# A shorter conv for one more block, with its weights loaded sooner, its softmax pieces and bands moved, and a warm-up in short matmuls

## Chip, cores, metric

One core of one Trainium2 chip. The metric is the device time of one execution in microseconds (us). All runs compared here are in the fast state. Times are medians; ratios are computed as the mean time of one kernel's fast runs over that of the other's of the same rounds, so they are not quite the ratios of the medians that are quoted.

## The reference, cut to what matters

A dynamic convolution (softmax weights over 7 taps, per token and head) feeds a feed-forward layer with a squared ReLU:

```python
w = softmax(weight_gen, axis=-1)                 # [8, 4096, 8 heads, 7 taps]
x_unf = x_pad[:, idx].reshape(B, S, K, H, 24)    # the last 7 tokens, 24 channels a head
x = einsum('bshk,bskhg->bshg', w, x_unf)         # -> 32768 tokens x 192
h = np.maximum(x @ w_in, 0.0)                    # 192 -> 2048
out = (h * h) @ w_out                            # 2048 -> 192
```

## The kernel before

Tokens go in blocks (the first two of 512, then of 1024); blocks count from 0, and the eighth is block 7. Names used below: a *unit* is 128 of the 2048 hidden channels for the block's 1024 tokens (`h`, six matmuls; relu on ScalarE; square `g` on VectorE for two units together). A *half sum* is 32 matmuls of the second layer into two PSUM banks `o0` and `o1`; after every second one ScalarE copies `o0` to SBUF and VectorE adds `o1` (`o_sb`). The *conv* of the next block multiplies x by *bands* (`bd`), which VectorE makes from the softmax weights (`wr`). A *piece* of softmax is a sum, a reciprocal and four or eight multiplications on VectorE, behind an exp on ScalarE. The kernel fixes by hand the order in which each engine gets its work, and this text holds that order:

```python
steady        = "MuMuuu" * 3 + "MuuuMCu"          # u unit, M half sum, C conv of the next block
steady_spread = "MuMuuu" * 2 + "MuCMuuu" + "MuMuuu"
...
TIMES = {                                          # softmax pieces: (block, before which unit)
    ...
    (1, 2): ((4, 2), (5, 1), (5, 15)),
    (2, 0): ((6, 1), (6, 15), (7, 0)),
    ...
}
...
us = {4: (7, 9), 6: (7, 9)}.get(j, (5, 9) if small else (1, 5))   # bands: before which units
if j + 1 >= FIRST_SPREAD:                          # FIRST_SPREAD = 8
    us = (1, 5)
```

The conv has two forms. A head has 24 channels and this kernel uses the array in groups of 32 columns, so in the long form a group straddles two heads and is written twice: 120 matmuls a block. In the short ("spread") form each head has a group of its own, and the 8 spare rows hold parts of the last two heads, filled in by DMA afterwards: 80 matmuls, but w_in must lie in a permuted order (`w_p`, loaded and then copied crosswise), and the conv must come early enough for the fill of y. Before, blocks 8 and later use it.

```python
copy(out=y[:, k0 : k0 + 2], in_=yp)                # ScalarE for one pair of slots, VectorE for the other
for p0 in range(0, P, 32):                         # four fill DMAs a block
    ...
    nc.sync.dma_start(out=y[p0 + G : p0 + 32, 0:NK], in_=y[r0 : r0 + G, NK])
```

The warm-up keeps TensorE busy until the first softmax weights are there:

```python
def spin(n):
    for i in range(n):
        nc.tensor.matmul(out=wp, lhsT=warm[:, 0:P], rhs=warm, start=True, stop=True)   # 512 columns
...
spin(21)
```

The softmax here doesn't subtract the row's maximum and nothing guards it: scores larger than these inputs give would overflow.

Of the kernel before, what the change touches and what calls it, by code (L numbers as in the profile page):

```python
# [9 lines left out]
def kernel(  # L10
# [26 lines left out]
    nc = tc.nc  # L37
# [3 lines left out]
    B, S, D = x.shape  # L41
    H, KK = weight_gen.shape[2], weight_gen.shape[3]
# [1 line left out]
    Dm = moe_w_out.shape[1]  # L44
    HK = H * KK
    G = D // H
    SPREAD = H - 2
    FIRST_SPREAD = 8
    HP = H // 2

    P = 128
    TB = 512
# [10 lines left out]
    RT = 64  # L63
    NK = D // RT
# [37 lines left out]
    PARTS = {0: (8, 8, 8, 8), 1: (8, 8, 16), 2: (16, 16)}  # L102
    v_big = const.tile([P, R + 2 * HALO, HP, SL, 2], f16, name="v_big")
    v_first = [
# [38 lines left out]
    def load_w_spread():  # L143

        def rows(head, k=None):
            a = moe_w_in[G * head : G * (head + 1)]
            return a if k is None else a.rearrange("(r k) c -> k r c", k=NK)[k]

        for e in (0, 1):
            for k in range(NK):  # L150
                for a, n, src in (
                    (0, G, rows(2 * k + e)), (G, RT // 2 - G, rows(SPREAD + e, k))
                ):
                    if k < 2:
                        p0 = RT * k + 32 * e + a
                        nc.gpsimd.dma_start(
                            out=w_p[p0 : p0 + n, :, 0, 0:NQ],
                            in_=src.rearrange("r (q c) -> r q c", q=WQ),
                        )
                    else:  # L160
                        for half in (0, 1):
                            p0 = RT * half + 32 * e + a
                            nc.gpsimd.dma_start(
                                out=w_p[p0 : p0 + n, :, 0, NQ:],
                                in_=src.rearrange("r (q h c) -> h r q c", q=WQ, h=2)[half],
                            )
# [124 lines left out]
    def rows(ap2d, t0, width):  # L291

        return bass.AP(
            tensor=ap2d.tensor, offset=ap2d.offset + t0 * width,
            ap=[[width, P], [STEP * width, NT], [1, width]],
        )
# [175 lines left out]
    def st_conv_spread(j):  # L472

        s0, n = BLOCKS[j]
        y = p_y.tile([P, NK + 1, TB], f16, name="y")
        y_t[j] = y
        for ks in ((NK, NK - 1), (0, 1)):
            yp = ps_h.tile([P, 2, TB], f32, name="yp", tag="h")
            k0 = min(ks)
            for k in ks:  # L480
                for i in range(NT):
                    a, b = bounds[i], bounds[i + 1]
                    for half in (0, 1):
                        s = s0 + half
                        hi = a + (STEP if tile_start(s, i) == starts[i] else b - a)
                        bd = bd_t[s][:, H * a : H * hi].rearrange(
                            "p (g c e) -> p g e c", g=HP, e=2
                        )
                        for e in (0, 1):
                            head = 2 * k + e  # L490
                            p0 = RT * half + 32 * e
                            c0 = min(G * head, D - 32)
                            nc.tensor.matmul(  # L493
                                out=yp[p0 : p0 + 32, k - k0, a:b],
                                lhsT=x_t[s][:, i, c0 : c0 + 32],
                                rhs=bd[:, head // 2, e, 0 : b - a],
                                start=True,
                                stop=True,
                                skip_group_check=True,
                                tile_position=(0, p0),  # L500
                            )
            copy = nc.vector.tensor_copy if k0 == 0 else nc.scalar.copy
            copy(out=y[:, k0 : k0 + 2], in_=yp)  # L503
        for p0 in range(0, P, 32):
            head = SPREAD + p0 // 32 % 2
            r0 = p0 + G * head - min(G * head, D - 32)
            nc.sync.dma_start(out=y[p0 + G : p0 + 32, 0:NK], in_=y[r0 : r0 + G, NK])

    def st_conv(j):

        if j >= FIRST_SPREAD:
            return st_conv_spread(j)
# [49 lines left out]
    def st_unit(j, u):  # L562

        w = w_p if j >= FIRST_SPREAD else w_i
        h = ps_h.tile([P, 2, TB], f32, name="h", tag="h")
# [91 lines left out]
    with nc.allow_low_precision("fp16 matmul pipeline"), tc.manual_schedule():  # L657
# [18 lines left out]
        warm = const.tile([P, TB], f16, name="warm")  # L676
# [3 lines left out]
        for v in v_first:  # L680
            nc.vector.memset(v, 0.0)

        wp = ps_o.tile([P, TB], f32, name="wp", tag="o0")

        def spin(n):
            for i in range(n):
                nc.tensor.matmul(out=wp, lhsT=warm[:, 0:P], rhs=warm, start=True, stop=True)

        s0, s1, s2 = parts[:3]
        spin(21)  # L690
        row_select()
        band_mask()
        s0.load(nc.sync)
# [35 lines left out]
        for q in range(4):  # L729
# [10 lines left out]
        plans = {  # L740
            0: "u P B1 u u u E1 C S1 u u M u u",
            1: "L3 u u B2 M E2 B3 u M E2 u u S2 S2 u M u C u M",
            2: "L4 u u u E3 M u u u M B4 u u u u M B5 S3 u u u u M u C E3 u",
            3: "L5 L6 u u u M S3 u u u M u M E4 u u B6 u M u M B7 u u u E4 M u M C S4 u",
        }


# [3 lines left out]
        def at(j, u, kind, *args):  # L751
# [5 lines left out]
        TIMES = {  # L757
            (1, 0): ((3, 15), (4, 0)),
            (1, 1): ((4, 15), (5, 0)),
            (1, 2): ((4, 2), (5, 1), (5, 15)),  # L760
            (2, 0): ((6, 1), (6, 15), (7, 0)),
            (2, 1): ((7, 9), (8, 9)),
            (3, 0): ((9, 9), (10, 0), (10, 9), (11, 9)),
# [2 lines left out]
        def exp_time(j, u):  # L766

            if u == 0:
                return j - 1, 12
            return j, {1: 0, 2: 1, 7: 3, 8: 4, 9: 4, 13: 12, 15: 8}[u]  # L770

        for n, s in enumerate(parts):
            k = n - min(m for m, p in enumerate(parts) if p.b == s.b)
# [4 lines left out]
        for n, s in enumerate(parts[4:], 4):  # L778
            b, f = s.b, s.fb
            k = n - min(m for m, p in enumerate(parts) if p.b == b)  # L780
# [8 lines left out]
        for j in range(len(plans), NBLK - 1):  # L789
            a = BLOCKS[j + 1][0]  # L790
            small = [p for p in parts if p.fb <= j + 1][-1].r == FIRST
            us = {4: (7, 9), 6: (7, 9)}.get(j, (5, 9) if small else (1, 5))
            if j + 1 >= FIRST_SPREAD:
                us = (1, 5)
            for n, u in enumerate(us):
                at(j, u, "B", a + n)
        for j in range(len(plans), NBLK):
            plan, u = [], 0
            for step in steady_spread if j + 1 >= FIRST_SPREAD else steady:
                if step == "u":  # L800
# [18 lines left out]
        def soft(s):  # L819
            lo, hi = next(s.softs)  # L820
            s.total(lo, hi)
            s.recip(lo, hi)
            s.scale(lo, hi, nc.vector)
            if hi < s.rh:
                return
            if s.r == FIRST:
                move_rows(s)
                after = parts[parts.index(s) + 1]
                if after.b == s.b and after.r > FIRST:
                    s.store(nc.sync)  # L830
            else:
                s.store(nc.sync)
                stored.add(s)
                for w in [w for w in waiting if w[0] is s]:
                    waiting.remove(w)
                    load_rows(w[1])
# [21 lines left out]
        for j in range(NBLK):  # L858
            if j + 2 < NBLK:
                load_rows(j + 2)  # L860
            if j == 1:
                for q in range(WQ):
                    cross_w_in(q)
            u = 0
            for step in plans[j].split():
                kind, n = step[0], int(step[1:] or 0)
                if kind == "u":
                    st_unit(j, u)
                    u += 1
                elif kind == "M":  # L870
                    next(mm2)
                elif kind == "C" and j + 1 < NBLK:
                    st_conv(j + 1)
                    if j == 0:
                        x_load(3)
                    elif j + 2 < NBLK:
                        for k in range(BLOCKS[j + 2][0], sum(BLOCKS[j + 2])):
                            x_load(k)
                    if j == 5:
                        load_w_spread()  # L880
                    elif j == 6:
                        cross_w_spread()
                elif kind == "E":
                    parts[n].exp(*next(parts[n].exps))
                elif kind == "S":
                    soft(parts[n])
                elif kind == "B":
                    st_bands(n)
                elif kind == "P":
                    select_rows(1, s0, ROW_ORDER[4:], (o1,))  # L890
                    copy_rows(1, ROW_ORDER[4:])
                elif kind == "L":
                    parts[n].load(nc.sync)


        j = NBLK - 1
# [44 lines left out]
```

## Time and profile before

| | before |
|---|---|
| time, median of 3 runs | 731.79 us (731.56 to 731.87) |
| span of the profiled run | 730.0 us |
| TensorE / VectorE / ScalarE busy | 99% / 86% / 84% |
| conv of block 7, start to next start | 1.53 us (120 matmuls); of block 8: 1.07 us (80) |
| a later block | 22.1 us |

Busy time says only that TensorE is the bound. What a change is worth is read from the order of time: where TensorE stands, and how long before that moment the engine that must release it had finished. The lines are in the prediction.

### The profile page before, as it was taken

The page shows a single profiled execution, that of the slowest core. Times are in us where ns is not written, and L with a number is a line of the kernel's source. Part 1 is how long each engine was busy: PE and PEld are TensorE (multiplying, and loading weights), DVE is VectorE, ACT ScalarE, POOL GpSimd, SP SyncE. Part 2 cuts the span into 40 slices and gives each one's busy share as a digit, 9 for nine tenths or more (in the row PEclk, how much of TensorE's full clock was granted, in tenths as well). Part 3 has the DMA queues.
Part 4 walks back from the last instruction along what each step waited for, and adds up shares of the span by engine and source line. Part 5 has one row for each costly group of instructions (what it writes and reads, how often), then busy time and mean ns, then how long its engine had stood idle before and what let it go on. Part 6 is the DMA issues. An engine that isn't in the chain of part 4 may idle for free.

```text
span 730.0 us, 30988 instructions
## 1 busy us (share of the span) xinstructions
PE 724.1 (99%) x14053; PEld 528.0 (72%) x14053; DVE 626.8 (86%) x836; ACT 612.2 (84%) x733; POOL 99.8 (14%) x145
## 2 busy tenths in 40 slices
PE   8999999999999999999999999999999999999998
PEld 4657788777777777777777777777777777777777
DVE  7998998998898988888988888988889988778753
ACT  5999888888888888888888888888888888888883
POOL 8131223321001100011001010010000110001000
PEclk9999999999999999999999999999999999999999
DMA  9555455685345452455432554343544325444012
GB/s 202 118 105 115 82 96 105 132 149 129 86 66 138 90 92 59 82 117 124 76 64 61 136 104 88 56 77 116 107 84 86 57 52 119 66 87 78 30 45 68
DMA packets 125984, 68.30 MB, mean 94 GB/s; under 512 B 85321, under 2 KB 122140, under 8 KB 125340
## 3 DMA queue, kind: packets, MB, share of 16 engines
q0 software_dynamic: 46192, 19.43, 22.9%
q1 hardware_dynamic: 79516, 46.79, 22.4%
q8 instruction: 110, 1.80, 1.1%
q14 instruction: 22, 0.18, 0.1%
q10 hardware_dynamic: 144, 0.10, 0.0%
HBM read 50.18 MB, written 28.70 MB: 108 GB/s over the span
## 4 chain that ended last, share of the span: by engine, by line
PE 98%; ACT 1%; DVE 0%; DMA 0%; issue 0%
PE o L621 47%; PE h L572 44%; PE yp L493 4%; PE h L557 2%; PE yp L527 1%; DMA wg<-in_weight_gen_dram 0%; PE yp L455 0%; ACT y L538 0%; DVE v_first L260 0%; PE pr L372 0%; ACT t L586 0%; DVE ssum L245 0%; ACT ex L238 0%; DVE rcp L252 0%; ACT wr L381 0%
## 5 line engine op out<-in xcount | busy, mean ns | idle before, releaser
L586 ACT ACTIVATE t<-h 128x1024 f16<-128x1024 f32 x512 | 496.4, 1026 | 60.3 <-PE h L572 58.8
L621 PEld LDWEIGHTS <-g 64*128 64x128 f16 (+1 forms) x8032 | 344.3, 94 | 55.0 <-issue 2.2
L621 PE MATMUL o<-w_o,g 64*128 64x192 f16 (+1 forms) x8032 | 380.1, 243 | 0.1
L590 DVE TENSOR_TENSOR g<-t 128x2048 f16<-128x2048 f16 (+1 forms) x287 | 307.4, 1105 | 30.1 <-ACT t L586 29.9
L572 PE MATMUL h<-y,w_p 64*128 64x512 f16 x2400 | 291.7, 376 | 0.0
L572 PEld LDWEIGHTS <-w_p 64*128 64x128 f16 x2400 | 113.9, 94 | 94.7
L395 DVE TENSOR_TENSOR bd<-wr,mask 128x4160 f16<-128x4160 f16 (+4 forms) x90 | 149.6, 1686 | 1.3 <-ACT wr L381 0.7
L637 DVE TENSOR_TENSOR o_sb<-o,o_sb 128x384 f32<-128x384 f32 x123 | 68.4, 556 | 61.1 <-ACT o_sb L635 60.1
L321 POOL DMA_DIRECT2D xt<-in_x_dram x63 | 52.6, 839 | 415.3 <-PE yp L493 362.5
L635 ACT COPY o_sb<-o 128x384 f32<-128x384 f32 x129 | 61.6, 477 | 45.9 <-PE o L621 45.1
L572 PE MATMUL h<-y,w_i 64*128 64x512 f16 x576 | 70.6, 376 | 0.3 <-ACT t L586 0.3
L572 PEld LDWEIGHTS <-w_i 64*128 64x128 f16 x576 | 30.3, 94 | 22.2 <-issue 1.6
L493 PEld LDWEIGHTS <-xt 128*32 128x32 f16 x2000 | 24.6, 95 | 10.6 <-issue 10.6
L260 DVE TENSOR_TENSOR v_big<-ex,rcp 128x112 f16<-128x112 f32 (+5 forms) x180 | 29.9, 237 | 1.7 <-DMA vd<-v_big 0.7
L503 DVE CAST y<-yp 128x1024 f16<-128x1024 f32 x25 | 30.4, 1218 | 0.0
L493 PE MATMUL yp<-bd,xt 128*32 128x104 f16 (+1 forms) x2000 | 28.4, 210 | 0.0
L238 ACT ACTIVATE ex<-wg 128x560 f32<-128x560 f32 (+4 forms) x38 | 25.9, 682 | 1.9 <-DMA wg<-in_weight_gen_dram 1.9
L245 DVE TENSOR_REDUCE ssum<-ex 128x80 f32<-128x560 f32 (+4 forms) x38 | 25.3, 666 | 1.3 <-ACT ex L238 1.3
L503 ACT CAST y<-yp 128x1024 f16<-128x1024 f32 x25 | 25.2, 1007 | 0.0
L252 DVE RECIPROCAL rcp<-ssum 128x80 f32<-128x80 f32 (+4 forms) x38 | 22.8, 600 | 1.3
L311 POOL DMA_DIRECT2D xt<-in_x_dram x7 | 3.9, 554 | 120.9 <-PE yp L493 109.4
L355 POOL DMA_DIRECT2D wr<-v_first x24 | 12.9, 560 | 25.1 <-DVE v_first L260 13.6
(41 smaller groups left out, 115.1 us busy)
## 6 DMA issues: line engine op xcount, KB each, us to landing
out_dram<-o_sb SPq DMA_DIRECT2D x63, 384.0 KB
xt<-in_x_dram POOLq DMA_DIRECT2D x42, 240.0 KB, 4.7
wg<-in_weight_gen_dram SPq DMA_DIRECT2D x4, 1064.0 KB
xt<-in_x_dram POOLq DMA_DIRECT2D x21, 192.0 KB, 5.2
wr<-vd SPq DMA_DIRECT2D x38, 80.0 KB
vd<-v_big SPq DMA_DIRECT2D x5, 512.0 KB
y<-y SPq DMA_DIRECT2D x100, 24.0 KB
wg<-in_weight_gen_dram SPq DMA_DIRECT2D x3, 616.0 KB
```

The costliest lines, as they stand in the source:

```text
L238: nc.scalar.activation(out=self.ex[:, lo:hi].rearrange("p r g k e -> p (r g) k e"), in_=self.wg[:, lo:hi].rearrange("p r (g e) k -> p (r g ...
L260: eng.tensor_tensor(out=bass.AP(tensor=v.tensor, offset=v.offset + lo * H * SL + lo % SL * 2 + g * SL * 2, ap=[list(v.ap[0]), [H * SL + 2, ...
L321: eng.dma_start(out=dst[:, first:last], in_=ap)
L395: nc.vector.tensor_tensor(out=bd_t[j][:, H * lo : H * (lo + len(tiles) * n)].rearrange("p (g m c) -> p g m c", g=shape[1], c=2 * SL), in0= ...
L493: nc.tensor.matmul(out=yp[p0 : p0 + 32, k - k0, a:b], lhsT=x_t[s][:, i, c0 : c0 + 32], rhs=bd[:, head // 2, e, 0 : b - a], start=True, sto ...
L503: copy(out=y[:, k0 : k0 + 2], in_=yp)
L572: nc.tensor.matmul(out=h[:, half], lhsT=w_in_chunk(w, u, slot, half), rhs=y_t[j][r0 : r0 + RT, k], start=(slot == 0), stop=(slot == NK - 1 ...
L586: nc.scalar.activation(out=t1[:, e], in_=h, func=ActF.Relu)
L590: nc.vector.tensor_tensor(out=g[:, a : e + 1], in0=t1[:, a : e + 1], in1=t1[:, a : e + 1], op=AluOp.mult)
L621: nc.tensor.matmul(out=oo[:, cc * Dm : (cc + 1) * Dm], lhsT=g[r0 : r0 + n, cc * P : (cc + 1) * P], rhs=w_o[r0 : r0 + n, fc, :], start=(fc ...
L635: nc.scalar.copy(out=o_sb, in_=o[0][:, c])
L637: nc.vector.tensor_tensor(out=o_sb, in0=o[1][:, c], in1=o_sb, op=AluOp.add)
```

## The change

Intent: take the short conv for block 7 too (40 matmuls fewer). That needs `w_p` a block sooner, the conv of block 7 after unit 8 of block 6 and therefore its bands at units 4 and 6, and for these the third softmax piece of part (1,2) at unit 11 of block 5 so that its rows are stored in time. Besides: an exp of the fourth part moves from before the last unit of block 2 to behind the second unit of block 3 (three units later; the recorded texts say two), the fill of y takes two DMAs instead of four (the window of odd heads starts 8 channels lower, so that the spare rows are neighbours), and the warm-up is cut in shorter matmuls. Each softmax piece takes its exp on ScalarE along: for the piece at unit 15 that is at unit 8, for the piece at unit 11 at unit 6.

```diff
-    FIRST_SPREAD = 8
+    FIRST_SPREAD = 7
 ... (window of the short conv, layout of w_p: cut)
-        for p0 in range(0, P, 32):
-            ...
-            nc.sync.dma_start(out=y[p0 + G : p0 + 32, 0:NK], in_=y[r0 : r0 + G, NK])
+        for r0 in (0, RT):
+            nc.sync.dma_start(
+                out=y[r0 + G : r0 + RT - G, 0:NK], in_=y[r0 + SPARE : r0 + RT - SPARE, NK]
+            )
 ...
-                nc.tensor.matmul(out=wp, lhsT=warm[:, 0:P], rhs=warm, start=True, stop=True)
+                nc.tensor.matmul(out=wp[:, 0:WARM], lhsT=warm[:, 0:P], rhs=warm[:, 0:WARM],  # WARM = 126
+                    start=True, stop=True)
-        spin(21)
+        spin(85)
 ...
-            2: "... M u C E3 u",
-            3: "L5 L6 u u u M S3 ...",
+            2: "... M u C u",
+            3: "L5 L6 u u E3 u M S3 ...",
 ...
-            (1, 2): ((4, 2), (5, 1), (5, 15)),
+            (1, 2): ((4, 2), (5, 1), (5, 11)),
 ...
-            us = {4: (7, 9), 6: (7, 9)}.get(j, (5, 9) if small else (1, 5))
-            if j + 1 >= FIRST_SPREAD:
+            us = {4: (7, 9), 6: (4, 6)}.get(j, (5, 9) if small else (1, 5))
+            if j + 1 > FIRST_SPREAD:
                 us = (1, 5)
 ... (load of w_p from the end of block 5 to its first unit, crossing from block 6 to block 5)
```

## The prediction

> **What bounds the kernel now.** I read the page first (busy shares, the chain that ended last), then the waits of each engine, then the order of time of TensorE (PE), VectorE (DVE) and ScalarE (ACT) around the places that the change touches. Blocks are counted from 0, so the eighth is block 7; a block is 16 hidden units (`h`, 0.65 us of PE each), eight half sums (`o`, 1.32 us each) and one conv (`yp`).
>
> ```profile
> PE 724.1 (99%) x14053; PEld 528.0 (72%) x14053; DVE 626.8 (86%) x836; ACT 612.2 (84%) x733; POOL 99.8 (14%) x145
> ...
> PE 98%; ACT 1%; DVE 0%; DMA 0%; issue 0%
> ```
>
> PE is 98% of the chain and never pauses for long: any PE time removed is gained, any new PE wait is lost. All waits of PE in the run:
>
> ```profile
> PE wp L687 <- DVE warm L678: 1.3, 1, 1.3
> PE pr L372 <- DVE v_first L260: 0.8, 2, 0.4
> PE h L572 <- ACT t L586: 0.3, 1, 0.3
> PE yp L455 <- ACT wr L381: 0.2, 1, 0.2
> ```
>
> So there is little to remove. But DVE is 86% busy, and every second half sum ends in a DVE add (`o_sb`, L637) that must free a PSUM bank before PE starts the half sum after next. The question is whether DVE still comes in time once work is moved on it. DVE from late block 5 (conv of block 6 is at 117.99, block 6 starts at 120.18):
>
> ```profile
> 114.75 2.35 DVE L590 TENSOR_TENSOR g<-t 128x2048 f16<-128x2048 f16 x2
> 117.45 1.83 DVE L590 TENSOR_TENSOR g<-t 128x2048 f16<-128x2048 f16 x2 [0.35 <-ACT t L586]
> 119.20 0.55 DVE L637 TENSOR_TENSOR o_sb<-o,o_sb 128x384 f32<-128x384 f32 x1
> 119.67 0.49 DVE L245 TENSOR_REDUCE ssum<-ex 128x48 f32<-128x336 f32 x1
> ...
> 124.17 0.56 DVE L637 TENSOR_TENSOR o_sb<-o,o_sb 128x384 f32<-128x384 f32 x1 [1.87 <-ACT o_sb L635]
> 124.65 0.61 DVE L245 TENSOR_REDUCE ssum<-ex 128x64 f32<-128x448 f32 x1
> ...
> 131.75 2.32 DVE L395 TENSOR_TENSOR bd<-wr,mask 128x4160 f16<-128x4160 f16 x1
> ```
>
> The reader is to see that DVE has 0.35 us idle before the add at 119.20, and 1.87 us only after it. PE at the same time, and at the two conv forms:
>
> ```profile
> 117.99 1.60 PE L527 MATMUL yp<-bd,xt 128*32 128x104 f16 x120
> 119.52 0.82 PE L572 MATMUL h<-y,w_i 64*128 64x512 f16 x6
> 120.18 1.48 PE L621 MATMUL o<-w_o,g 64*128 64x192 f16 x32
> ...
> 131.96 0.81 PE L572 MATMUL h<-y,w_i 64*128 64x512 f16 x6
> ```
> ```profile
> 155.25 1.13 PE L493 MATMUL yp<-bd,xt 128*32 128x104 f16 x80
> 156.32 0.92 PE L621 MATMUL o<-w_o,g 64*128 64x192 f16 x18
> ```
>
> [...] 6 hidden-unit matmuls of 512 columns, two at a time on half the rows, take 0.65 us, 216 ns a pair. [...] the row selections (128x128 weights, 64 columns) follow each other at 29 ns[...]. [...] the trace shows about 0.09 us on the way into each conv (6 matmuls take 0.74 for 0.65), the same for both forms.
>
> **The change, part by part.**
>
> *Short conv for block 7.* 120 matmuls in 1.53 us (140.54 to 142.07) become 80 in 1.07 us (155.25 to 156.32): gain 0.46 us, all on the PE path.
>
> *Exp of the fourth part two units later.* At 51.8 ACT copies the conv of block 3 (1.50 us), then runs this exp (starts 53.18), and only then the relu at 53.60 that frees the buffer for the PE unit at 54.67; PE had been ready at 54.09. Without the exp the relu starts 0.42 us sooner, so gain 0.42. Two units later the relus have some 0.1 us to spare; I give nothing back.
>
> *Warm-up.* 21 x 512 = 10752 columns become 85 x 126 = 10710. [...] to 4.1 us (before, matmuls start every 427 ns until then) and 55 ns each after, the short ones end near 7.3 us; the first real matmul waits for `v_first` until 7.73. Gain 0.
>
> *w_in loaded sooner, and the fill of y in two DMAs for four per block.* The 16 weight loads follow the row moves that end on POOL at 104.27; at 0.58 us each they end before the x load at 119.87, and the DMA rings stood idle from 112 to 119. The crossing then lands near 130 (6.9 us after issue), needed at 144. Nothing on the path.
>
> *What moves on DVE.* The built program shows the order of instructions. Here I expect losses, three of them.
>
> A. The third softmax piece of part (1,2) (1.73 us of DVE: 119.67 to 121.40) goes from behind the add at 119.20 to ahead of it, after the `g` at 114.75. Idle of 0.35 takes some: the add ends 1.73 - 0.35 = 1.38 later, at 121.1 for 119.75. PE needs that bank at its second matmul of the half sum at 120.18: stall 0.9.
>
> B. Block 6 takes the schedule in which the conv comes after unit 8, that is 12.5 us after the block's start (132.7), not at its end. Its bands must be ready by then. DVE's chain starts at the add of 124.17, which PE itself releases, and now holds: softmax piece from 124.65, 1.97 without the old 0.66 wait (126.62); two `g` at 1.13 (128.88); band 2.23 (131.11); add 0.46 (131.57); `g` 1.13 (132.70); band 2.3 (135.0). The conv's third matmul reads the second band: stall 135.05 - 132.7 = 2.35. About 1.0 of this appears already in the half sum at 130.64, which waits for the add of 131.57. A moves both sides alike, so it doesn't shrink B. In block 7 before, the same chain has no softmax piece inside and its two `g` end the bands at 154.78, 0.47 ahead of the conv.
>
> C. Before, the conv at the end of block 6 gave DVE 1.5 us and more for the softmax piece of unit 15 (142.29, finished with the last `g` at 144.96, 2.23 after the block's start at 142.73). Now no conv stands there. By the pattern of block 8 (start 164.82), the `g` of unit 14 ends 1.7 after the start; then piece 1.97, then the `g` of unit 15 0.68: 4.36. The second half sum reads it 1.97 + 7 x 0.165 = 3.12 after the start: stall 1.25. The conv of block 8 then just finds its bands (13.7 against 13.8).
>
> Sum: 731.79 - 0.46 - 0.42 + 0.9 + 2.35 + 1.25 = 735.4.
>
> **Rivals.** (1) *Clean gain*: DVE keeps up, no new wait; 731.79 - 0.88 = 730.9. For it: the placements look tuned, and before has not one PE wait on DVE after the start. Against it: the adds above have only 0.43 us to spare at 120.18, and the sums exceed that. (2) *The loads collide*: the weight loads share the rings with the row moves that band 10 waits for at 107.43; if these land 1 us later the band, and with it A, grow by up to 0.5: 735.9. Against it: the moves were all issued by 104.95. (3) *Warm-up slower*: [...] the 29 ns pairs speak against it. (4) *Only some of A, B, C*: ACT is late elsewhere, so DVE may have idle that I did not see; half of them gives 733.1.
>
> **Range and chances.** I give the three stalls together some 70%, partial ones 15%, the clean gain 15%. Predicted 734.8, a little under the sum for the latter; 8 in 10 between 730.7 and 736.3, which holds the clean gain at its edge. Two per cent is 14.6 us, more than any of these: faster 0.005, same 0.985, slower 0.01.
>
> **What would show it.** In the profile after: 80 matmuls for block 7's conv, in 1.07 us of PE work; the PE wait of 0.3 us on the relu near 54 gone or down to 0.1; the first row selection still at 7.7 us; new PE waits on DVE `o_sb` near 120 (0.9) and 131 (1.0), on DVE `bd` near 135 (1.3), and on DVE `g` about 2 to 3 us into block 7 (1.25); from block 9 on the period of 22.1 us unchanged. The prediction is wrong if PE shows no waits on DVE between 118 and 150, or if the span is under 731; and if PE waits there for DMA (`w_p`, `xt`, `y`), the second rival is right.

## The result, and the profile after

The changed kernel took 736.74 us (median of 6 runs, 736.09 to 739.13) against 731.83 us (731.56 to 731.99): ratio 1.0071, 95% interval 1.0057 to 1.0085. It is slower by 4.9 us, and its runs spread over 3 us where those of before spread over 0.4. Within 2%, but above the stated range, which ended at 736.3.

The profiled run (736.18 us, span 734.2) on the page, to be held against the two page lines in the prediction:

```profile
PE 725.1 (99%) x14077; PEld 532.9 (73%) x14077; DVE 627.8 (86%) x837; ACT 612.5 (83%) x732; POOL 99.2 (14%) x145
...
PE 96%; DVE 2%; ACT 1%; issue 1%; DVEq 0%
```

Busy shares tell nothing; the chain does: 2% of it, some 15 us, now runs over VectorE. All waits of TensorE after (total us, times, longest):

```profile
PE o L622 <- DVE o_sb L638: 1.5, 2, 0.9
PE wp L689 <- DVE warm L679: 1.3, 1, 1.3
PE o L622 <- DVE g L591: 1.2, 1, 1.2
PE yp L494 <- DVE bd L396: 1.1, 1, 1.1
PE pr L373 <- issue: 0.7, 1, 0.7
PE yp L456 <- ACT wr L382: 0.2, 1, 0.2
```

The wait of 0.3 us on a relu is gone. Four new ones on VectorE and one on "issue" have come. VectorE after, in order of time (start, us, instruction), answering to the same stretch of before:

```profile
114.97 1.22 DVE L591 TENSOR_TENSOR g<-t 128x2048 f16<-128x2048 f16 x1
116.11 0.50 DVE L246 TENSOR_REDUCE ssum<-ex 128x48 f32<-128x336 f32 x1
...
117.75 2.96 DVE L591 TENSOR_TENSOR g<-t 128x2048 f16<-128x2048 f16 x3
120.63 0.55 DVE L638 TENSOR_TENSOR o_sb<-o,o_sb 128x384 f32<-128x384 f32 x1
...
125.63 0.61 DVE L246 TENSOR_REDUCE ssum<-ex 128x64 f32<-128x448 f32 x1
...
132.12 0.55 DVE L638 TENSOR_TENSOR o_sb<-o,o_sb 128x384 f32<-128x384 f32 x1
...
133.72 2.32 DVE L396 TENSOR_TENSOR bd<-wr,mask 128x4160 f16<-128x4160 f16 x1
```

The moved piece (116.11) stands ahead of the add, which ends at 121.18 instead of 119.75. The chain from the piece at 125.63 to the second band ends at 136.04. TensorE after, the four lines that begin with such a wait, and the stop at the start:

```profile
12.05 0.23 PE L373 MATMUL pr<-v_first,sel 128*128 128x64 f16 x2
13.01 0.58 PE L373 MATMUL pr<-v_first,sel 128*128 128x64 f16 x14 [0.73 <-issue]
...
121.23 1.48 PE L622 MATMUL o<-w_o,g 64*128 64x192 f16 x31 [0.66 <-DVE o_sb L638]
...
132.72 1.48 PE L622 MATMUL o<-w_o,g 64*128 64x192 f16 x31 [0.86 <-DVE o_sb L638]
...
136.09 1.12 PE L494 MATMUL yp<-bd,xt 128*32 128x104 f16 x78 [1.09 <-DVE bd L396]
...
150.09 0.34 PE L622 MATMUL o<-w_o,g 64*128 64x192 f16 x4 [1.15 <-DVE g L591]
```

Each begins within 0.1 us of the end of the VectorE instruction named. To book the time I took the start of each of the 249 stretches of half sums in both traces and their difference (after less before):

| where | change of the difference, us |
|---|---|
| start, until the first half sum (18.83 before) | +0.73 |
| exp later, block 3 | -0.40, then +0.14 |
| blocks 4 and 5, small steps (one of -0.29, from a stop that the trace of before has there and that of after has not; see the section on 85 matmuls) | -0.34 |
| A: first half sum of block 6 | +0.83 |
| B with the short conv: block 6 to start of block 7 | +1.94 (a wait of 2.4, a conv shorter by 0.46) |
| C: second half sum of block 7 | +1.32 |
| all later blocks | 0.0 |
| sum | +4.2 (spans 734.2 and 730.0) |

### The profile page after: what moved, and what is told of

The parts are those of the page before. It is cut to its first block, busy times and chain, and to the rows that moved or that the text cites. A ratio compares the mean times of both kernels' runs of the same rounds, so it can differ in the third digit from the quotient of the medians.

```text
span 734.2 us, 30929 instructions
## 1 busy us (share of the span) xinstructions
PE 725.1 (99%) x14077; PEld 532.9 (73%) x14077; DVE 627.8 (86%) x837; ACT 612.5 (83%) x732; POOL 99.2 (14%) x145
## 4 chain that ended last, share of the span: by engine, by line
PE 96%; DVE 2%; ACT 1%; issue 1%; DVEq 0%
PE o L622 46%; PE h L573 43%; PE yp L494 4%; PE h L558 2%; DVE g L591 1%; PE wp L689 1%; PE yp L528 1%; DVE bd L396 1%; ACT t L587 0%; DVE v_big L261 0%; DVE o_sb L638 0%; PE yp L456 0%; PE pr L373 0%; ACT o_sb L636 0%; DVE rcp L253 0%
## 5 line engine op out<-in xcount | busy, mean ns | idle before, releaser
L573 PE MATMUL h<-y,w_p 64*128 64x512 f16 x2496 | 303.4, 376 | 0.0
L573 PEld LDWEIGHTS <-w_p 64*128 64x128 f16 x2496 | 118.5, 94 | 98.5
L573 PE MATMUL h<-y,w_i 64*128 64x512 f16 x480 | 59.0, 376 | 0.0
L573 PEld LDWEIGHTS <-w_i 64*128 64x128 f16 x480 | 26.6, 94 | 17.3 <-issue 1.2
```

The source lines that it names most:

```text
L573: nc.tensor.matmul(out=h[:, half], lhsT=w_in_chunk(w, u, slot, half), rhs=y_t[j][r0 : r0 + RT, k], start=(slot == 0), stop=(slot == NK - 1 ...
```

## The experiments

Theory: three waits on VectorE (A, B, C) take 4.5 us, and the warm-up costs what is missing. Rivals: the loads of `w_p` collide with other transfers, and the missing time lies elsewhere.

### Warm-up undone in the changed kernel

```diff
-        spin(85)      # 126 columns
+        spin(21)      # 512 columns
```

> The changed kernel with the old warm-up (21 matmuls of 512 columns); all else as changed. Theory (three waits on VectorE, and besides them a slower start from the 85 short matmuls): the three waits stay (0.8, 2.3 and 1.3 us), the 0.7 us at the start goes, so 735.2 to 735.6, and the runs agree within 0.5 us as those of before did, instead of spreading over 3 us. Rival (the missing time lies in the middle, the warm-up is neutral): 736.2 to 737 with the same spread.

Measured 735.58 us (735.40 to 736.00), before 731.99, ratio 1.0051. The stop is gone, the three waits are as they were. It is 3.59 us over the kernel before of its rounds; the sum of the prediction without its hedge (735.4) was 3.62 over.

### Warm-up alone in the kernel before

```diff
-        spin(21)      # 512 columns
+        spin(85)      # 126 columns
```

> The kernel before with only the warm-up in 85 short matmuls. Theory (slower, varying start): 0.5 to 2 us over before, runs spread by over 1 us, the first hidden unit of block 0 begins after 13.2 us instead of 12.7. Rival (neutral, as predicted): within 0.2 us of before.

Measured 733.07 us (732.60 to 735.89), before 731.99, ratio 1.0021. The first hidden unit starts at 13.70 instead of 12.71, with a wait on "issue" of 1.05 us in the row selections. So the warm-up is not neutral.

### Exp alone, twice

```diff
-            2: "... M u C E3 u",
-            3: "L5 L6 u u u M S3 ...",
+            2: "... M u C u",
+            3: "L5 L6 u u E3 u M S3 ...",
```

> The kernel before with only the exp of the fourth part two units later. Theory: 0.40 us less, 731.4, from the unit at 54.67 that starts 0.4 sooner. Rival (given back within block 3, where the relus come later): 731.8.

> The kernel before with only the exp later, again, since its gain of 0.40 us at block 3 was seen in the trace but not in the times. Theory (a real gain, hidden by the moment at which the clock is granted, which differs from run to run): 0.1 to 0.5 us under before, the wait near 54 gone. Rival: no difference.

Measured 731.80 us against 731.99, ratio 1.0000 (0.9988 to 1.0012); again, 731.92 against 731.92, ratio 1.0000 (0.9987 to 1.0012). The times tell nothing. The trace of the second run shows why the gain is smaller than 0.42:

```profile
52.16 2.96 PE L572 MATMUL h<-y,w_i 64*128 64x512 f16 x24
...
58.20 1.68 PE L621 MATMUL o<-w_o,g 64*128 64x192 f16 x32
```

The 24 hidden-unit matmuls now run in one piece, 0.39 us saved; but TensorE then comes to the half sum at 58.20 before VectorE's add is done, and this takes 1.68 us by the view where before it took 1.50: 0.14 given back. What is left, 0.25 us, is less than the start moved from run to run: TensorE ran at half speed until a moment between 3.9 and 6.8 us into the profiled spans (in the kernel before, the warm-up matmuls start 427 ns apart until 4.1 us and 216 ns apart after), and where that came late (6.84 in the first of these two runs) the first half sum came 0.24 us later.

### Loads and fill alone, then the crossing put back

The kernel before with the new layout, the fill in two DMAs, and loads and crossing of `w_p` a block sooner; block 7 still in the long form. Then the same with this line undone:

```diff
-                    if j == 5:
+                    if j == 6:
                         cross_w_spread()
```

> The kernel before with the permuted w_in loaded and crossed a block sooner and the fill of y in two DMAs instead of four, but block 7 still in the long form and every softmax piece, band and exp where it was. Theory (all hidden): within 0.2 us of before. Rival (the loads delay the row moves of band 10): 0.3 to 1 us slower, with a longer wait of a band near 107 us.

> As the run with loads and crossing a block sooner, but the crossing of w_in left where it was, after the conv of block 7. Theory (its loss came from the crossing[...]): within 0.3 us of before, the store of v_big lands in 5.1 us again and no band waits for DMA near 132. Rival (the loads themselves cost): 0.5 to 1.3 us over before as in that run.

Measured 733.19 us (732.23 to 733.28), before 731.99, ratio 1.0013 (1.0001 to 1.0025); with the crossing late, 732.01 against 731.92, ratio 1.0001. The expectation of nothing was wrong for the first, though not where the rival put it: band 10 did not wait. VectorE in the profiled run (the mildest of the five), with the crossing early:

```profile
126.95 0.83 DVE L261 TENSOR_TENSOR v_big<-ex,rcp 128x112 f16<-128x112 f32 x4 [1.07 <-DMA vd<-v_big]
...
132.35 2.33 DVE L396 TENSOR_TENSOR bd<-wr,mask 128x4160 f16<-128x4160 f16 x1 [0.48 <-DMA wr<-vd]
```

and with it late:

```profile
126.97 0.83 DVE L261 TENSOR_TENSOR v_big<-ex,rcp 128x112 f16<-128x112 f32 x4 [0.90 <-DMA vd<-v_big]
...
131.97 2.32 DVE L396 TENSOR_TENSOR bd<-wr,mask 128x4160 f16<-128x4160 f16 x1
```

The crossing (two copies of 384 KB, issued at 121.7) runs beside the store of part (1,2) and the rows made of it; a band then waits 0.48 us for DMA, and in this trace TensorE waits 0.18 us for an add near 136. The store itself took 5.5 us, until the rows that wait for it were issued, with the crossing early and 5.35 with it late, so it is hardly slowed here. This points to the crossing but does not prove it: the runs of the first kernel fall in two groups (732.23 and 732.29; 733.19, 733.20 and 733.28), only a run of the faster group was profiled, and the intervals of the two ratios overlap (the second's is 0.9989 to 1.0014). The loads themselves, in the idle stretch after 104 us (GpSimd issues nothing from 104.27 to 119.87 in the trace of before), cost nothing that these runs show.

### Third piece put back

All of this group start from the changed kernel with the old warm-up (735.58 us).

```diff
-            (1, 2): ((4, 2), (5, 1), (5, 11)),
+            (1, 2): ((4, 2), (5, 1), (5, 15)),
```

> The changed kernel with the old warm-up and the third softmax piece of part (1,2) back at unit 15 of block 5. Theory (wait A is this piece standing ahead of the add): the wait of 0.8 us at the first half sum of block 6 goes; but its store now lands late again, the next softmax piece waits some 0.6 us for it and the waits at the half sum near 131 and at the conv of block 7 grow by as much together, from 2.3 to about 2.9: net 735.2 to 735.6. Rival (the waits are independent): 734.7.

Measured 739.72 us (738.77 to 739.79), before 731.73, ratio 1.0105: a miss by 4 us. Wait A went, as expected. But B's chain now stood still twice for DMA, and TensorE 5 us:

```profile
127.89 0.83 DVE L261 TENSOR_TENSOR v_big<-ex,rcp 128x112 f16<-128x112 f32 x4 [2.09 <-DMA vd<-v_big]
...
133.11 2.33 DVE L396 TENSOR_TENSOR bd<-wr,mask 128x4160 f16<-128x4160 f16 x1 [2.13 <-DMA wr<-vd]
```
```profile
135.96 2.71 PE L622 MATMUL o<-w_o,g 64*128 64x192 f16 x31 [5.13 <-DVE o_sb L638]
```

I had counted the store's landing at 5.1 us, as before; here it took 6.5 (issued 121.43, rows issued 127.94). Beside the same crossing it took 5.5 in the run with the loads alone and 5.3 in the last run of this group (121.34 to 126.61), so the crossing alone does not explain the 6.5; its cause is not shown. And TensorE's clock was granted at half from 133.07, in the middle of TensorE's wait, for 6.8 us (mean granted clock 0.51 from 133 to 140 us): the 31 matmuls took 2.71 us for the 1.48 of the same lines elsewhere. The piece at unit 11 was thus needed, and A is its price.

### First piece of part (2,0) behind the conv

```diff
-            (2, 0): ((6, 1), (6, 15), (7, 0)),
+            (2, 0): ((6, 9), (6, 15), (7, 0)),
```

> The changed kernel with the old warm-up and the first softmax piece of part (2,0) moved from unit 1 to unit 9 of block 6, behind the conv. Theory (wait B is VectorE's chain from the add near 125 to the second band): 1.97 us leave the chain, but its second square then waits for a relu, so the half sum near 131 waits 0.4 instead of 1.0 and half sum and conv together 1.8 instead of 2.3; A and C stay: about 735.0. Rival (the bands wait for their rows from DMA, or for something else): B unchanged, 735.5.

Measured 735.25 us (734.91 to 735.37), ratio 1.0048. In the trace the stretch from the half sum near 131 to the end of the conv is 0.50 us shorter than in the changed kernel, A and C stay. As the chain predicts, 1.97 us taken out of it give only 0.5 (TensorE's two waits on `o_sb` are 1.0 us in all, for 1.5 in the changed kernel), for by its count the next square waits for its relu. The time does not decide: 735.25 lies between the 735.0 of the theory and the 735.5 of the rival, and over the kernel before of the same rounds it is 3.52 us, for 3.59 without this edit.

### Second piece of part (2,0) behind the conv

```diff
-            (2, 0): ((6, 1), (6, 15), (7, 0)),
+            (2, 0): ((6, 1), (6, 9), (7, 0)),
```

> The changed kernel with the old warm-up and the second softmax piece of part (2,0) moved from unit 15 to unit 9 of block 6. Theory (wait C is this piece standing ahead of the last square of block 6): the wait of 1.2 us at the second half sum of block 7 goes, A and B stay: 734.2 to 734.4. Rival (VectorE is short of time there in any case): the wait turns up at a band or an add of block 7 and the time stays above 735.

Measured 734.12 us (733.81 to 734.98), ratio 1.0034. TensorE's waits on VectorE are now these:

```profile
PE o L622 <- DVE o_sb L638: 1.4, 2, 0.9
...
PE yp L494 <- DVE bd L396: 1.1, 1, 1.1
```

The wait on `g` is gone, the difference steps by 1.32 us at that place, and nothing takes its place. C is this piece.

### A try at the gain without the waits

```diff
+            first = "MuMuuu" * 3 + "MuCMuuu"      # block 6: conv after unit 12
+            # softmax pieces and bands of block 6 as before; both copies of this conv on ScalarE
```

> A try at the gain without the waits: short conv of block 7 and early loads as changed, but softmax pieces and bands of block 6 where they were before, the conv after unit 12 of block 6 (when the bands are just ready), both its copies on ScalarE, old warm-up, exp later as changed. Theory: A and B gone, C down to 0.2 to 0.5 us, the fill of y just in time: 0.1 to 0.6 us under before. Rival (VectorE's work in block 6 is too much for any place of a conv before unit 15): waits of over 1 us remain, no faster than before.

Measured 735.55 us (734.01 to 736.31), ratio 1.0049: a miss. A and C are gone, but a band waited 0.96 us for its rows, the half sum at 136.64 waited 0.66 us for VectorE's add, and the fill of y came late:

```profile
147.08 1.27 PE L573 MATMUL h<-y,w_p 64*128 64x512 f16 x5 [2.19 <-DMA y<-y]
```

I had counted 2.2 us from issue to landing. That is the shortest fill of this trace (2.2 to 5.5 us, median 4.4); issued at 141.67 and 142.37, this one took some 5. After this wait of 2.2 us the clock was at half for 3.4 us more: 30 matmuls of the half sum at 147.76 took 2.83 us, where 32 took 1.48 at 143.20.

### What it is about 85 matmuls

Two warm-ups in the kernel before: 43 matmuls of 250 columns, and 15 of 512 followed by 70 of 16.

```diff
-        spin(21)      # 512 columns
+        spin(43)      # 250 columns            (first run)
+        spin(85)      # 15 x 512, 70 x 16      (second run)
```

> The kernel before with its warm-up in 43 matmuls of 250 columns, so 44 instructions more instead of 128. Theory (PE stops at its 449th instruction because the next block of instructions[...] takes some 2.4 us to come, and 85 short matmuls bring PE there too soon): the 449th instruction is then in the conv of block 1 after 16 us, more than 4 us after the fetch: no stop, within 0.3 us of before. Rival (shorter matmuls warm the array up worse, or are slower as such): a third of the loss or more, 0.3 to 1 us over before.

> The kernel before with 15 warm-up matmuls of 512 columns as they were and then 70 of 16 columns: 85 in number again, but most of the columns in long ones. Theory (the number of instructions counts): PE stops at its 449th instruction, in the row selections near 12 to 13 us, for 0.7 to 1.3 us, and the time is 0.7 to 1.5 us over before. Rival (the 126 columns count): no stop, within 0.3 us of before.

Measured 731.50 us (731.26 to 731.89) against 731.92, ratio 0.9995 (0.9981 to 1.0009), and 733.21 us (732.94 to 734.10), ratio 1.0020. TensorE in the second, in the same row selections:

```profile
12.58 0.23 PE L372 MATMUL pr<-v_first,sel 128*128 128x64 f16 x2
13.54 0.58 PE L372 MATMUL pr<-v_first,sel 128*128 128x64 f16 x14 [0.72 <-issue]
```

and in the first, where nothing stops:

```profile
11.99 0.64 PE L372 MATMUL pr<-v_first,sel 128*128 128x64 f16 x16
```

So it is the number of instructions, not their width: a wait of 0.72 us with 85 matmuls of which 70 are narrow, none with 43. The whole loss of the second kernel is not the stop, though: its first half sum comes 1.26 us later than before, and 0.58 of this was there before the stop, because its spin lasted until 8.88. In all three kernels with 85 warm-up matmuls TensorE stops after 446 loads and matmuls of the trace (the recorded texts speak of the 449th instruction) and goes on 2.4 us after a 16 KB transfer on the instruction queue (q8 of the page) begins: 10.58 to 13.01, 10.84 to 13.29, 11.16 to 13.54. With 21 matmuls such a transfer begins at 13.21 and the 447th is due only at 16.55. The kernel before has a stop of the same kind elsewhere, which the list of waits in the prediction does not show:

```profile
97.26 1.85 PE L621 MATMUL o<-w_o,g 64*128 64x192 f16 x32
```

This half sum takes 1.85 us for 1.48: TensorE stops for 0.36 us and goes on at 98.61, with its 3517th load or matmul, 2.35 us after a 16 KB transfer began. With the two semaphore instructions in between counted, this is 12 x 256 instructions behind the place of the other stop. In the last kernel below, with 22 warm-up matmuls more, TensorE stops (for 0.30 us, until 97.40) before its 3517th again, which is then 44 instructions sooner in the program. So the stops keep to instruction numbers, here 12 x 256 apart, and not to a place in the program.

The transfers on that queue are of 16 KB each (1.80 MB in 110 packets, 16.4 KB each, in the trace of the second kernel). That TensorE stands there for instructions that have not yet come is the author's inference from these times, not seen.

### The changed kernel without the stop, and the two harmless parts together

```diff
-        spin(85)      # 126 columns, changed kernel
+        spin(43)      # 250 columns            (first run)
```

The second run is the kernel before with `spin(43)` and the exp later.

> The changed kernel with its warm-up in 43 matmuls of 250 columns instead of 85 of 126. Theory (the stop at the 449th instruction explains both the missing time and the spread): no stop near 12 us, the three waits on VectorE as they are, 734.8 to 735.6, and the runs within 0.7 us of each other. Rival (something else in the changed kernel varies): 736 or more, or runs spread over more than 1.5 us.

> The kernel before with the warm-up in 43 matmuls of 250 columns and the exp of the fourth part later, nothing else. Theory (0.4 us from the other places of instruction fetches, 0.25 from the exp): 0.4 to 0.8 us under before. Rival (both within what the moment of the clock's grant shifts): no difference to be told.

Measured 735.38 us (735.12 to 735.65) against 732.05, ratio 1.0045; and 731.22 us (730.98 to 731.93), ratio 0.9990 (0.9977 to 1.0002). Without the stop the changed kernel's runs lie within 0.53 us, and its three waits are unchanged. The last version has the lowest median of all, 0.8 us under the kernel before, but its interval takes in no difference.

## Why the prediction was right or wrong

- **Short conv, gain 0.46**: right. It takes 1.07 us of matmuls once its bands are there.
- **Exp, gain 0.42, "I give nothing back"**: 0.40 gained, 0.14 given back at an add of VectorE that had just been in time. I checked the relus and not the add.
- **A 0.9, B 2.35 and C 1.25**: right in place, in releaser and in size: 0.83, 2.4 and 1.32. Undoing them one at a time confirms C fully, B in its structure (0.5 predicted, 0.50 in the trace), and A in that it went with the piece. One word is wrong there: the add must be done before the next half sum, not "the half sum after next"; the working takes it right.
- **Warm-up, "Gain 0"**: this is the step that failed. I compared when the spin ends (7.3) with when the first weights are there (7.73), and so weighed columns only. (The 55 ns a matmul of that sum lie on the line through the 29 ns of 64 columns and the 216 of 512 in the trace of before.) In the profiled run the clock came later (6.3 us, for 4.1 before) and the spin ended at 8.34, which cost almost nothing (0.05 us at the first conv); what cost was the spin's 128 more instructions: with them TensorE stands still for 0.73 us in that trace, by the inference above because the next instructions are not yet there. A stop of this kind, 0.36 us at 98.6, stood already in the trace of before, but not in the list of waits that I went by. Rival (3) had the warm-up slower too, but by slower pairs, which the trace of after refutes: pairs of 126 columns follow each other in 55 ns from 6.4 us on (103 to 106 before that). The size: 1.1 us in the kernel before (733.07 against 731.99), 1.3 to 1.6 in the changed one (4.91 us over the kernel before with the stop, 3.59 and 3.33 without it, each against the same rounds).
- **Loads "nothing on the path"**: right in the changed kernel, whose trace has no TensorE wait on DMA; wrong for the same loads without the moved piece, where something, probably the crossing, cost about 1 us in three runs of five (733.19 against 732.01; the cause is not shown). With the third piece at unit 11 no such wait is left, and A is paid for that.
- **The number**: 731.79 - 0.88 + 4.5 = 735.4 was what the steps said, and the kernel without the stop takes 735.4. I then lowered it to 734.8 for the chance that tuned placements are good; that hedge had no reading behind it, and with the missing term it put the result outside.

What stays open: two runs, one in each of the two kernels with 85 matmuls of 126 columns, were 2 to 3 us slower than their fellows (739.13 and 735.89), both with a mean granted clock of 0.998. A second stretch at half clock would do that, by the author's estimate from the two profiled runs that waited longest (3.4 us at half and a mean of 0.998, 6.8 us and 0.995), but no such run was profiled, and the third kernel with 85 matmuls has none.

## What to carry to other kernels

Where one engine is at 99%, a piece of work put on another engine is not free because that one is at 86% (here three waits on VectorE, 4.5 us): list, for each hand-over to the full engine, when it is due and what now stands ahead of it in the same queue, and add up from the last moment at which that queue was forced to wait. A gain of 0.5 us that needs work before a deadline instead of after it can cost several times itself (0.46 gained by the short conv, 4.5 lost). And count instructions as well as columns at the start of a program: a warm-up in four times as many matmuls moved TensorE into a stop of 0.7 to 1.05 us (85 for 21), while half as many short ones cost nothing that the runs show (43; ratio 0.9995).

## What the traces show of the hardware

- Pairs of a weight load and a matmul: in the trace of the changed kernel pairs of 126 columns start 55 ns apart from 6.4 us on, and pairs of 64 columns 29 ns.
- Clock after a wait of TensorE: after one of 2.19 us (conv after unit 12) the clock was at half for 3.4 us; in one of 5.13 us (third piece put back) it went to half 2.2 us after the wait began, for 6.8.
- Stops by instruction number: with 85 warm-up matmuls TensorE stood still for 0.7 to 1.05 us when it reached its 447th load or matmul sooner than 2.4 us after a transfer of 16 KB began, and for 0.36 us at its 3517th in the kernel before.
- Time to landing of a DMA beside others: the rows that wait for the store of 256 KB were issued 2.8 us after it in the changed kernel, 5.1 in the kernel before and 6.5 with the third piece put back; a fill copy of 48 KB landed in 4.2 us in the changed kernel (median; 2.7 to 6.0).
